# The first unit of a fused attention and expert-mixture kernel: scores copied straight from PSUM, masks on GpSimd, and a new order of the first steps

## The chip, the cores and the metric

The kernel runs on one core of one Trainium2 chip. The metric is the device time of one execution in microseconds (us); three executions give a median of 1105.48 us (1104.85 to 1106.03). All data are fp32.

## The reference

The first block is a recurrent attention. For each of 4 batches and 8 heads a 40 by 40 state is carried over 768 tokens; the second block takes the attention's output, with heads side by side, through four experts and adds them up with weights.

```python
for t in range(S):                                  # S = 768, head_dim = 40
    y[:, :, t] = einsum('bhd,bhde->bhe', r_t, state)
    Sa = einsum('bhde,bhe->bhd', state, a_t)
    state = state * w_t[:, :, None, :] - einsum('bhd,bhe->bhde', Sa, b_t)
    state = state + einsum('bhd,bhe->bhde', v_t, k_t)

x = y as (3072, 320)
p = domain_probs / (domain_probs.sum(-1) + 1e-9)    # 4 experts
for e in range(4):
    out += p[:, e] * (relu(x @ w1[e]) @ w2[e])      # 320 -> 1024 -> 320
```

## The kernel before

**Units.** The tokens are cut into 12 chunks of 64, and the four batches into two pairs. One chunk of one pair is a unit, so there are 24 units, numbered u = 0 to 23; one unit gives 128 rows of x. The recurrence within a chunk is turned into small matrix products and one triangular solve for each head.

**The steps of a unit.** `within(q)` is a generator; each `run(ws[u], 1)` takes it to its next `yield`. It transposes the decays into `G`, scans them, transposes them back by TensorE (`pg`), divides (`gp`, a VectorE reciprocal), scales `n_tok`, `k_tok` and `AT`, transposes the first two by TensorE (`pNT`, `pKT`), and forms the score products `pfe` (for the solve), `pe` (masked into `ET`) and `pc` (masked into `VC`). `pev` multiplies `ET` with the values. `substitute(q, eng)` is the triangular solve: `blocks` gathers the 32 by 32 diagonal blocks of the scores, one VectorE transpose lays them out as `M`, and a loop over 16 pairs of columns fills `Z`. Units 0 and 1 solve on VectorE, later ones on GpSimd. `merge(q)` transposes the result into `Qc` and `QTc`, and joins blocks by the products `pY` and `pQ`. `step(q, xT)` then uses the carried state: products `psat`, `pst`, `pxr`, `pdy`, the output `Y`, the next state, and `pxT`, which places the 40-wide heads into the rows `xT` of x.

**The mixture.** `mixture_of_unit(q)` puts pieces into the list `todo`: `ups(e)` (x times w1 into `ph`, 64 matmuls of 128 columns and four activations to `hs`) and `down(e)` (`po`, 16 matmuls of 320 columns, and one VectorE addition into `osb`). `mix(n)` issues the next n pieces. They are the bulk of TensorE's work, and from the second unit on they fill its waits. Weights come by `load_piece()` (w1, in pieces that alternate over buffers) and `load_w2(e)`.

**What sets the order.** A list scheduler places the instructions of each engine. `tc.keep_in_program_order(ins)` ties an instruction behind the one traced before it on its engine. While `in_order[0]` is set (units 0 to 5), every matmul and transpose is tied, so TensorE runs exactly in the order in which the code calls `run`, `mix` and `keep_warm`. `keep_warm(n)` issues n products of the identity with itself, whose result nobody reads. The order of the first two units is written out by hand at the end of the kernel; SyncE's loads stand there too.

**PSUM.** Tiles by the tag `big` share five banks, those by `mm` three. Before, the target of `keep_warm` is a `big` tile.

The order by hand that the change touches, from the first unit's scores to the second unit's solve, cut to its TensorE and VectorE work, before the change:

```python
run(ws[0], 2); keep_warm(12)                     # scores of unit 0
substitute(units[0], nc.vector, scores_of(0))    # scores_of: masks ET
run(ws[0], 1); m, s = merge(units[0]), begin_step(0)
run(m, 1); run(ws[0]); keep_warm(4); run(norm, 1)
run(ws[1], 1); keep_warm(3); run(ws[1], 1); run(m)
run(ws[1], 1); run(s, 3); run(ws[1], 1); run(s, 1)
run(ws[1], 1); run(s); run(ws[1], 2); mixture_of_unit(units[0])
substitute(units[1], nc.vector, scores_of(1), during_second)
# during_second: mix(1) at j = 0 and 14, the rest of ws[1] at j = 4
```

Of the kernel before, what the change touches and what calls it, by code (L numbers as in the profile page):

```python
# [15 lines left out]
def kernel(  # L16
# [218 lines left out]
    def go(moves, eng=None):  # L235
        for move in moves:
            move(eng or nc.sync)
# [10 lines left out]
    tc.keep_in_program_order(nc.vector.tensor_copy(out=mask_up[:], in_=upf[:]))  # L248
    ins = nc.vector.transpose(out=unit_cols[:], in_=dealt(diagf[:, None, :].to_broadcast([P, H, Q])))
    tc.keep_in_program_order(ins)  # L250
    go(load_raw(units[0], "W"))
    load(units[0], "WBK")
    go(load_raw(units[0], "A"), nc.scalar)
    for x in "VR":
# [82 lines left out]
    def quarter(q):  # L337
        return slice(Q * q, Q * q + Q)
# [63 lines left out]
    def within(q):  # L402
# [3 lines left out]
        def pin(ins, also=False):  # L406
            if q.u <= PADDED or also:
                tc.keep_in_program_order(ins)
# [2 lines left out]
        G = sb.tile([P, 2 * NJ * L + 1], FP32, name="G", tag="G", bufs=3)  # L411
        q.G = Gv = G[:, 0:2 * NJ * L].rearrange("p (c t) -> p c t", t=L)
        ahead = G[:, 1:2 * NJ * L + 1].rearrange("p (j i t) -> p i j t", i=2, t=L)
        for i in range(2):
            pin(turn_raw(ahead[:, i], n["rawW"][:, NJ * i:NJ * i + NJ, :]))
        q.gl = sb.tile([P, 2 * NJ, 1], FP32, name="gl", tag="gl", bufs=4)
        pin(nc.vector.tensor_tensor(out=q.gl[:], in0=G[:, L::L][:, :, None], in1=first[:, :, 0:1], op=ALU.mult))
        pin(nc.vector.memset(Gv[:, :, 0:1], 0.0))
        q.AT = sb.tile([P, 2 * NJ, L], FP32, name="AT", tag="AT", bufs=2)

        def turn_rv():
# [11 lines left out]
            return VT  # L433

        if q.u == 1:
            yield
            VT = turn_rv()
            yield
        pin(nc.vector.tensor_tensor_scan(
            out=G[:, 0:2 * NJ * L], data0=G[:, 0:2 * NJ * L],  # L440
            data1=first[:].rearrange("p c i -> p (c i)"), initial=0.0, op0=ALU.mult, op1=ALU.add,
        ))
        nc.vector.tensor_tensor(out=q.gl[:], in0=q.gl[:], in1=Gv[:, :, L - 1:L], op=ALU.mult)
        if q.u < 2:
            pin(turn_raw(q.AT[:], n["rawA"][:]))
        yield

# [12 lines left out]
        def token_V():  # L460
            return n["paddedV"][:, :, 0:D] if q.u < PADDED else n["V"][:]

        def causal_scores(VT):
            pc = quadrants(banks("pc"), 0, BY_TOKENS, L, lambda j, s, i: (
                d_half(j, s), i, j, of_slots(VT, d_half(j, s), j, i, D), of_slots(q.RT, d_half(j, s), j, i, D),
            ))
            for r in range(2):
                pin(causal(of_d_half(q.VC[:, :, D:D + L], r), pc[r]), q.start)

        q.K, q.N = k_tok(), n_tok()  # L470
        ins = nc.vector.scalar_tensor_tensor(
# [9 lines left out]
        pin(ins)  # L481
        q.VC = VCs()
        if q.u > 0:
            nc.scalar.copy(out=q.VC[:, :, 0:D], in_=token_V())
        if q.u >= PADDED:
            VT = turn_rv()
        yield
# [13 lines left out]
            s, i ^ s, j, of_slots(q.AT, s, j, i), of_pairs(NT, s, j, i),  # L501
        ))
        def copy_F():
            q.F = sb.tile([P, H, L], FP32, name="F", tag="F", bufs=1)
            for s in range(2):
                nc.scalar.copy(out=of_slot(q.F[:], s), in_=pf[s])  # L506
# [13 lines left out]
            yield  # L520

        ET = ETs()
        for s in range(2):
            pin(causal(of_slot(ET[:], s), pe[s]), q.start)
        yield

# [9 lines left out]
        yield  # L536

        if q.u == 0:
            causal_scores(turn_rv())
        yield  # L540

    def substitute(q, eng, between=None, during=None):

        blocks = sb.tile([P, H, Q], FP32, name="blocks")
        for i in range(P // Q):
            move = nc.scalar.copy if i >= 2 else nc.vector.tensor_copy
            tc.keep_in_program_order(move(out=blocks[quarter(i)], in_=q.F[quarter(i), :, quarter(i % 2)]))  # L547
        q.below = belows()
        for i in (1, 3):
            tc.keep_in_program_order(nc.gpsimd.tensor_copy(out=q.below[quarter(i)], in_=q.F[quarter(i), :, 0:Q]))  # L550
        M = sb.tile([P, Q, Q], FP32, name="M")
        cols = blocks[:].rearrange("p h c -> p c h")[:, :, None, :].to_broadcast([P, Q, 4, H])
# [5 lines left out]
        on_diag = M[:].rearrange("p c r -> p (c r)")[:, Q + 1::2 * (Q + 1)]  # L558
        tc.keep_in_program_order(nc.vector.memset(on_diag, 0.0))

        Z = sb.tile([P, 4, Q // 4, Q], FP32, name="Z")
        q.Z = Z[:, 0]
        by_second = Z[:, 1:3].rearrange("p x k r -> p (x k) r")
        below = M[:].rearrange("p c r -> p (c r)")[:, 1::2 * (Q + 1)]
# [4 lines left out]
        ins = nc.vector.tensor_tensor(out=pairs[:, :, 0, :], in0=pairs[:, :, 0, :], in1=by_second, op=ALU.add)  # L569
        tc.keep_in_program_order(ins)  # L570
        run(between)
        at_once = eng is nc.vector
        for x in (0, 3) if at_once else (0,):
            tc.keep_in_program_order(eng.tensor_copy(out=Z[:, x], in_=unit_cols[:]))
        for j in range(0, Q, 2):
            if during:
                during(j)
# [21 lines left out]
    def merge(q):  # L599


        Qc = sb.tile([P, H, Q], FP32, name="Qc", tag="q", bufs=2)
        QTc = sb.tile([P, H, Q], FP32, name="QTc", tag="q", bufs=2)
        tc.keep_in_program_order(nc.vector.transpose(out=dealt(Qc[:]), in_=q.Z))  # L604
        tc.keep_in_program_order(
            nc.vector.transpose(  # L606
                out=QTc[:].rearrange("p h r -> p (h r)"), in_=Qc[:].rearrange("p h c -> p (h c)"),
            )
        )
        q.QT = QTs()  # L610
        for i in range(P // Q):
            ins = nc.gpsimd.tensor_copy(out=q.QT[quarter(i), :, quarter(i % 2)], in_=QTc[quarter(i)])  # L612
            tc.keep_in_program_order(ins)
        yield

        def two_heads(name, lhsT, rhs, to):
            p = big(name)
            for n in range(NJ):
                for r in range(2):
                    matmul(  # L620
                        out=p[half(r), n * 2 * Q:(n + 1) * 2 * Q], lhsT=lhsT[half(r), 2 * n:2 * n + 2, :],
                        rhs=rhs[half(r), 2 * n:2 * n + 2, :], start=True, stop=True,
                    )
            for r in range(2):
                for y in range(2):
                    src = p[quarter(2 * r + y), 0:H * Q].rearrange("p (n two t) -> p n two t", two=2, t=Q)[:, :, y, :]
                    nc.scalar.copy(out=of_slot(to[quarter(2 * r)], y), in_=src)  # L627

        Y = Ys()
        two_heads("pY", q.below, QTc, Y)  # L630
        yield

        two_heads("pQ", Qc, Y, q.QT[:, :, quarter(1)])
        yield

    def step(q, xT):
# [31 lines left out]
        if not q.end:  # L668
# [2 lines left out]
                i ^ s, i, j, q.QT[half(i ^ s), head(j, s), :], RH[half(i ^ s), head(j, s), 0:D],  # L671
            ))
        SaT = sb.tile([P, NJ, 2, L], FP32, name="SaT", tag="step", bufs=3)
        for x in range(2):
            nc.scalar.copy(out=SaT[:, :, x, :], in_=psa[x])
        if not q.end:
            for x in range(2):
                for i in range(2):
                    s = i ^ x
                    nc.scalar.copy(out=of_slot(SX[half(i)], s)[:, :, 0:D], in_=pst[x][half(i)])  # L680
        yield

        p = banks("pxr")
# [34 lines left out]
            )  # L718
        if not q.start:
            nc.vector.tensor_tensor(out=Y[:], in0=Y[:], in1=Gv, op=ALU.mult)  # L720
        if not q.end:
            gl = q.gl[:].rearrange("p (j i) o -> p j i o", i=2)
            for i in range(2):
                x = st[i][:, :, 0:D]
                nc.vector.tensor_tensor(out=x, in0=pdy[i][:, :, 0:D], in1=x, op=ALU.add)
                nc.vector.tensor_tensor(out=x, in0=x, in1=gl[:, :, i, :].to_broadcast([P, NJ, D]), op=ALU.mult)
        yield

        if placed:
# [7 lines left out]
        for h in range(0 if placed else H):  # L737
            lo = h * D
            while lo < (h + 1) * D:
# [7 lines left out]
                    )  # L747
                lo = hi
        yield

    def up_last(k, xT, n):

# [48 lines left out]
    def mixture_of_unit(q):  # L801
# [3 lines left out]
        def ups(e):  # L805
            ph = []

            def lead():
                if not ph:
                    ph.append(up_last(at + 2 * e, q.xT, P))  # L810

            def piece():
                lead()
                hs[e] = [up_main(at + 2 * e, q.xT, P, ph[0])]
                hs[e].append(up_main(at + 2 * e + 1, q.xT, P, up_last(at + 2 * e + 1, q.xT, P)))
                used(at + 2 * e + 2)
                if q.u == 0 and e + 2 < E:
                    load_w2(e + 2)

            piece.lead = lead  # L820
            return piece
# [176 lines left out]
        q.xT = chunks_x[q.c][:, :, q.bp * P:(q.bp + 1) * P]  # L998
        return step(q, q.xT)

    warm = big("warm")

    def keep_warm(n):

        for _ in range(n):
            ins = matmul(out=warm[:, 0:P], lhsT=ident[:], rhs=ident[:], start=True, stop=True)
            tc.keep_in_program_order(ins)

    in_order[0] = True
# [5 lines left out]
    run(ws[0], 1)  # L1015
    keep_warm(10)
    run(ws[0], 1)
    run(ws[1], 1)
    for x in "VR":
        load_padded(units[1], x)  # L1020
    load(units[1], "WBK")
    go(load_raw(units[1], "A"))
    go(load_raw(units[2], "W"))
    load_probs()
    run(ws[0], 2)
    keep_warm(12)

    def scores_of(u):
        run(ws[u], 1)
        yield  # L1030

    substitute(units[0], nc.vector, scores_of(0))
    run(ws[0], 1)
    set_pick()
    m, s = merge(units[0]), begin_step(0)
    run(m, 1)
    run(ws[0])
    keep_warm(4)
    run(norm, 1)
    run(ws[1], 1)  # L1040
    keep_warm(3)
    load(units[2], "W")
    for x in "VR":
        load_padded(units[2], x)
    load_piece()
    load_piece()
    run(ws[1], 1)
    go(load_raw(units[2], "A"))
    load_w2(0)
    load_piece()  # L1050
    load_piece()
    run(m)
    run(ws[1], 1)
    run(s, 3)
    run(ws[1], 1)
    run(s, 1)
    run(ws[1], 1)
    run(s)
    load(units[2], "BK")
    load_w2(1)  # L1060
    load_piece()
    run(ws[1], 2)
    mixture_of_unit(units[0])

    def during_second(j):
        if j in (0, 14):
            mix(1)
        if j == 4:
            run(ws[1])
        if j == 12:  # L1070
            run(norm)

    substitute(units[1], nc.vector, scores_of(1), during_second)
    m, s = merge(units[1]), begin_step(1)
    run(m, 1)
    run(ws[2], 1)
# [144 lines left out]
```

## Time and profile before

| what | value |
|---|---|
| median of three executions | 1105.48 us (1104.85 to 1106.03) |
| the profiled execution, its own time | 1102.3 us |
| its span, first to last instruction | 1100.6 us |
| mean granted TensorE clock | 0.991 |
| TensorE matmuls busy | 1070.0 us (97%) |
| VectorE busy | 756.6 us (69%) |
| ScalarE busy | 353.0 us (32%) |
| GpSimd busy | 502.9 us (46%) |
| stage 0 to 20 us: matmuls busy, clock | 13.59 us, 1.00 |
| stage 20 to 40 us | 13.11 us, 0.65 |
| stage 40 to 60 us | 18.94 us, 0.93 |
| stage 60 to 80 us | 19.13 us, 1.00 |

Times in this text that name a moment are us from the span's start. In lists of instructions the columns are start, length, engine, line and operation, what is written from what, the number of instructions, and in brackets the idle time before the first of them with what ended it. Lines of a table by stage give the stretch, its length, and for each engine the busy time with the number of instructions, then the granted clock, the mean share of the DMA engines and GB/s. The profiled execution lies 3.2 us below the median of the others.

### The profile page before, as it was taken

How to read it: one execution, taken by the hardware profiler on the slowest of the kernel's cores; microseconds unless marked ns; L12 is line 12 of the kernel's file. 1: busy time of each engine (PE TensorE's matmuls, PEld its weight loads, DVE VectorE, ACT ScalarE, POOL GpSimd, SP SyncE). 2: the span in 40 equal slices, each digit the busy share in tenths (PEclk: the TensorE clock that was granted, in tenths of full speed). 3: DMA queues.
4: the chain of work that ended last, by engine and by line, in shares of the span. 5: the costliest groups of instructions: out<-in, count | busy, mean ns of one | idle time of the engine just before them, and what ended most of it. 6: DMA issues, size and time to landing. Idle time of an engine off the chain costs nothing.

```text
span 1100.6 us, 38528 instructions
## 1 busy us (share of the span) xinstructions
PE 1070.0 (97%) x16102; PEld 955.8 (87%) x16102; DVE 756.6 (69%) x1551; ACT 353.0 (32%) x956; POOL 502.9 (46%) x1274
## 2 busy tenths in 40 slices
PE   6799899999999999999999999999999999999998
PEld 6677788789998999898999989989998989988887
DVE  7766668887777776767767768767767677543343
ACT  2432444223233233243233242332332432321110
POOL 5106677753463653743734635636537437430000
PEclk9799999999999999999999999999999999999999
DMA  7776545425345363354353444443552532222320
GB/s 117 226 247 138 136 103 117 119 55 136 98 111 127 98 140 97 94 146 103 93 144 94 102 121 104 116 120 84 127 123 65 147 85 67 98 69 82 104 76 13
DMA packets 268868, 122.18 MB, mean 111 GB/s; under 512 B 213736, under 2 KB 242072, under 8 KB 268696
## 3 DMA queue, kind: packets, MB, share of 16 engines
q1 hardware_dynamic: 265416, 119.12, 43.0%
q8 instruction: 127, 2.08, 0.8%
q10 hardware_dynamic: 3280, 0.61, 0.3%
q14 instruction: 45, 0.37, 0.1%
HBM read 111.79 MB, written 3.93 MB: 105 GB/s over the span
## 4 chain that ended last, share of the span: by engine, by line
PE 81%; DVE 7%; POOL 5%; ACT 3%; issue 2%; DMA 1%; SPq 0%; ACTq 0%; DVEq 0%; POOLq 0%
PE ph L76 35%; PE p L76 28%; POOL Z L593 3%; PE pdy L76 3%; PE psat L76 2%; PE pxr L76 2%; POOL Z L580 2%; PE prn L76 1%; PE pfe L76 1%; PE pQ L76 1%; PE po L76 1%; PE pc L76 1%; DVE Z L590 1%; PE pY L76 1%; DVE M L553 1%
## 5 line engine op out<-in xcount | busy, mean ns | idle before, releaser
L76 PE MATMUL ph<-xT,w1p 128*128 128x256 f32 (+3 forms) x3040 | 446.3, 377 | 4.0 <-issue 3.9
L76 PEld LDWEIGHTS ph<-xT,w1p 64*64 64x64 f32 (+1 forms) x3040 | 338.5, 162 | 72.7 <-issue 29.0
L593 POOL TENSOR_TENSOR Z<-Z 128x31 f32<-128x31 f32 (+7 forms) x704 | 260.0, 369 | 55.2
L897 DVE TENSOR_TENSOR a<-hs 128x512 f32<-128x512 f32 x220 | 151.8, 707 | 104.7 <-ACT hs L778 104.7
L580 POOL TENSOR_TENSOR Z<-M,Z 128x62 f32<-128x62 f32 (+7 forms) x352 | 144.1, 409 | 132.3 <-DVE M L569 106.4
L778 ACT ACTIVATE hs<-ph 128x512 f32<-128x512 f32 (+1 forms) x208 | 115.3, 564 | 226.5 <-PE ph L76 225.4
L76 PE MATMUL p<-sums,a 128*128 128x160 f32 x1056 | 164.9, 299 | 0.0
L76 PEld LDWEIGHTS p<-sums,a 128*128 128x128 f32 x1056 | 152.8, 190 | 2.2
L791 DVE SCALAR_TENSOR_TENSOR osb<-p,gate,osb 128x320 f32<-128x320 f32 (+1 forms) x243 | 108.1, 481 | 57.8 <-PE p L76 53.6
L550 POOL COPY below<-F 32x256 f32<-32x256 f32 x48 | 22.8, 475 | 198.7 <-ACT F L506 197.0
L76 PE MATMUL p<-w,a 128*128 128x160 f32 x704 | 105.9, 301 | 0.2 <-ACT hs L778 0.2
L76 PE MATMUL p<-w,hs 128*128 128x160 f32 x704 | 102.9, 299 | 0.0
L76 PEld LDWEIGHTS p<-w,hs 128*128 128x128 f32 x704 | 100.2, 190 | 2.2
L76 PEld LDWEIGHTS p<-w,a 128*128 128x128 f32 x704 | 98.3, 190 | 3.0 <-ACT hs L778 3.0
L612 POOL COPY QT<-QTc 32x256 f32<-32x256 f32 x96 | 51.7, 539 | 76.9 <-DVE QTc L606 67.7
L553 DVE STREAM_TRANSPOSE M<-blocks 128x1024 f32<-128x1024 f32 x24 | 47.4, 1977 | 38.1 <-ACT blocks L547 37.9
L700 ACT COPY RS<-pxr 64x256 f32<-64x256 f32 x88 | 32.2, 366 | 105.2 <-DVE SX L400 43.1
L451 DVE RECIPROCAL gp<-gp 128x320 f32<-128x320 f32 x24 | 51.6, 2151 | 0.7
L535 ACT COPY EV<-pev 64x160 f32<-64x160 f32 x96 | 23.1, 286 | 89.7 <-PE pev L76 89.3
L604 DVE STREAM_TRANSPOSE Qc<-Z 128x256 f32<-128x256 f32 x24 | 15.0, 627 | 46.2 <-POOL Z L593 46.1
L627 ACT COPY QT<-pQ 32x128 f32<-32x128 f32 x96 | 24.6, 256 | 59.9 <-PE pQ L76 58.2
L659 ACT COPY SN<-prn 128x256 f32<-128x256 f32 x44 | 14.9, 372 | 78.6 <-DVE RH L654 78.6
(149 smaller groups left out, 1357.5 us busy)
## 6 DMA issues: line engine op xcount, KB each, us to landing
w1p<-in_moe_w_dram SPq DMA_DIRECT2D x95, 512.0 KB
w1p<-in_moe_w_dram SPq DMA_DIRECT2D x190, 64.0 KB
w<-in_moe_w_dram SPq DMA_DIRECT2D x4, 1280.0 KB
sums<-in_moe_w_dram SPq DMA_DIRECT2D x9, 512.0 KB
natW<-in_w_dram SPq DMA_DIRECT2D x48, 80.0 KB
natB<-in_b_dram SPq DMA_DIRECT2D x48, 80.0 KB
natK<-in_k_dram SPq DMA_DIRECT2D x48, 80.0 KB
out_dram<-osb SPq DMA_DIRECT2D x46, 80.0 KB
```

What stands on the lines that cost most here:

```text
L76: return stated(nc.tensor.matmul(**k))
L451: pin(nc.vector.reciprocal(out=gp[:], in_=gp[:]))
L535: nc.scalar.copy(out=of_slot(q.EV[half(p)], i ^ p)[:, :, 0:D], in_=pev[i][half(p)])
L553: ins = nc.vector.transpose(out=M[:], in_=cols)
L580: ins = eng.tensor_tensor(out=Z[:, 1:3, 0:n, j + 1:Q], in0=M[:, j:j + 2, None, j + 1:Q].to_broadcast([P, 2, n, m]), in1=Z[:, here, 0:n, j: ...
L593: eng.tensor_tensor(out=z[:, 0], in0=z[:, 0], in1=z[:, x], op=ALU.add)
L612: ins = nc.gpsimd.tensor_copy(out=q.QT[quarter(i), :, quarter(i % 2)], in_=QTc[quarter(i)])
L627: nc.scalar.copy(out=of_slot(to[quarter(2 * r)], y), in_=src)
L700: nc.scalar.copy(out=RS[half(s), x ^ s::2], in_=prs[x][half(s)].rearrange("p (j i) t -> p j i t", i=2),)
L778: nc.scalar.activation(out=h[:, i * HF // 2:(i + 1) * HF // 2, 0:n], in_=ph[i][:], func=ACTF.Relu,)
L791: nc.vector.scalar_tensor_tensor(out=to, in0=p, scalar=sc, in1=to, op0=ALU.mult, op1=ALU.add)
L897: nc.vector.tensor_tensor(out=t[:], in0=x, in1=y, op=op)
```

## The change

1. The four loads of the first unit's decays alternate between SyncE's queue and ScalarE's queue, ahead of the other loads there.
2. `within` turns the second unit's `V` and `R` first, its decays in the next step and `AT` in a third, before the scan, and has one more `yield`.
3. Units 0 and 1 have no SBUF copy `F` of their scores. `blocks` is copied from the PSUM banks `pf` in eight parts (five by VectorE, three by ScalarE), and `below` by four ScalarE copies in place of two GpSimd copies from `F`.
4. In unit 0 the two masks (`ET` and the right half of `VC`) are no longer predicated VectorE copies. ScalarE copies the scores to SBUF, and GpSimd's `affine_select` writes them masked (`selected`).
5. In unit 0 the two copies of the unit columns into `Z` stand ahead of the gathering of `blocks` instead of after the masks.
6. In unit 0 half of the copies out of `pY`, `pQ`, `psat` and `pst` go to VectorE.
7. The next state of unit 0 is computed in a step of its own, later.
8. The spare products write a tile of the tag `mm`, and there are 16, 10, 19, 5, 8 and 6 of them where there were 16, 10, 12, 4 and 3.
9. The order by hand changes. The first unit's masks, its `V` and `R`, the gate's transposes and the second unit's `V` and `R` are all called ahead of the first `merge`. The second unit's scan stands behind the whole first step; the first piece of the mixture, `ups(0)`, stands ahead of the second unit's `n_tok`, and no longer inside its solve. Loads move with it: the third unit's decays go behind two weight pieces.

```diff
-    go(load_raw(units[0], "W"))
+    for n, move in enumerate(load_raw(units[0], "W")):
+        tc.keep_in_program_order(move(nc.scalar if n % 2 else nc.sync))
...
         if q.u == 1:
+            VT = turn_rv()
             yield
-            VT = turn_rv()
+        for i in range(2):
+            pin(turn_raw(ahead[:, i], n["rawW"][:, NJ * i:NJ * i + NJ, :]))
+        if q.u == 1:
+            yield
+            pin(turn_raw(q.AT[:], n["rawA"][:]))
...
+        def selected(to, spread, data):
...
+            for s in range(2):
+                tc.keep_in_program_order(nc.scalar.copy(out=spread(copied, s), in_=data[s]))
+            for i in range(2):
+                nc.gpsimd.affine_select(
+                    out=to[part(i)], in_=copied[part(i)], pattern=[[0, H], [1, L]], compare_op=ALU.is_gt, fill=0.0,
+                    base=0, channel_multiplier=-1,
+                )
...
+        if q.u == 0:
+            unit_columns()
+        if q.pf:
+            for n, (i, s) in enumerate((i, s) for i in range(P // Q) for s in range(2)):
+                move = nc.scalar.copy if n >= 5 else nc.vector.tensor_copy
+                to, src = of_slot(blocks[quarter(i)], s), q.pf[s][quarter(i), :, quarter(i % 2)]
+                tc.keep_in_program_order(move(out=to, in_=src))
+            if q.u > 0:
+                copy_below(q)
...
-    warm = big("warm")
+    warm = ps.tile([P, P], FP32, name="warm", tag="mm", bufs=3)
...
     run(ws[0], 2)
-    keep_warm(12)
-
-    def scores_of(u):
-        run(ws[u], 1)
-        yield
-
-    substitute(units[0], nc.vector, scores_of(0))
-    run(ws[0], 1)
     set_pick()
+    keep_warm(19)
+    substitute(units[0], nc.vector)
+    run(ws[0], 3)
+    keep_warm(5)
+    run(ws[0])
+    run(norm, 1)
+    keep_warm(8)
+    run(ws[1], 1)
+    keep_warm(6)
     m, s = merge(units[0]), begin_step(0)
     run(m, 1)
-    run(ws[0])
-    keep_warm(4)
-    run(norm, 1)
-    run(ws[1], 1)
-    keep_warm(3)
...
     run(ws[1], 1)
+    go(load_raw(units[2], "W"))
+    run(m, 1)
+    run(ws[1], 1)
...
     run(m)
-    run(ws[1], 1)
-    run(s, 3)
+    run(s, 4)
     run(ws[1], 1)
     run(s, 1)
     run(ws[1], 1)
+    mixture_of_unit(units[0])
+    mix(1)
+    run(ws[1], 1)
     run(s)
+    run(ws[1], 1)
...
     run(ws[1], 2)
-    mixture_of_unit(units[0])
...
     def during_second(j):
-        if j in (0, 14):
-            mix(1)
         if j == 4:
             run(ws[1])
         if j == 12:
             run(norm)
+        if j == 14:
+            mix(1)
```

## The prediction

> **What bounds the kernel now.** I read the page first, then the table by stage, then the instructions of each engine over the first 75 us.
>
> ```profile
> PE 1070.0 (97%) x16102; PEld 955.8 (87%) x16102; DVE 756.6 (69%) x1551; ACT 353.0 (32%) x956; POOL 502.9 (46%) x1274
> ...
> PEclk9799999999999999999999999999999999999999
> ```
>
> TensorE is 97% busy and its clock is low in one slice, the second (27.5 to 55 us). From about 75 us the order of the work is unchanged, so the change is worth what it moves the moment at which unit 2's first product, `pg`, can start behind the same pieces of the mixture. Now that is 69.75. The table by stage (stretch, length, busy and count of PE, PEld, DVE, ACT, POOL, clock, DMA share, GB/s):
>
> ```profile
> 18.00:20.30 2.30, 0.00 (x1) 0.03 (x1) 2.15 (x6) 0.00 (x0) 0.00 (x0) 1.00 0.71 129
> 22.50:36.10 13.60, 8.19 (x72) 6.98 (x74) 12.03 (x35) 4.38 (x13) 2.40 (x4) 0.50 0.60 145
> 36.10:39.50 3.40, 2.49 (x36) 1.80 (x35) 0.58 (x2) 2.05 (x8) 0.00 (x0) 0.99 0.63 112
> 39.50:43.00 3.50, 3.05 (x95) 2.76 (x96) 2.81 (x4) 1.79 (x6) 1.30 (x2) 0.51 1.00 355
> 48.50:54.30 5.80, 5.23 (x81) 4.58 (x72) 4.64 (x9) 2.98 (x8) 0.84 (x2) 1.00 0.84 231
> 54.30:69.75 15.45, 14.95 (x128) 11.15 (x128) 14.28 (x50) 2.49 (x8) 2.26 (x4) 1.00 0.74 232
> ```
>
> Up to 48.5 TensorE waits for VectorE's chain, with a halved clock for 17 us; after it TensorE has 0.6 + 0.5 us idle up to 69.75. VectorE's list gives the first solve:
>
> ```profile
> 13.61 0.92 DVE L241 STREAM_TRANSPOSE G<-rawW 128x256 f32<-128x256 f32 x2
> ...
> 16.21 1.99 DVE L553 STREAM_TRANSPOSE M<-blocks 128x1024 f32<-128x1024 f32 x1 [0.16 <-ACT blocks L547]
> ...
> 19.73 0.76 DVE L400 COPY_PREDICATED ET<-mask_up,pe 128x256 f32<-128x256 int32 x2
> 20.39 0.49 DVE L574 COPY Z<-unit_cols 128x256 f32<-128x256 f32 x2
> 20.80 0.22 DVE L580 TENSOR_TENSOR Z<-M,Z 128x62 f32<-128x62 f32 x1
> ```
>
> and TensorE's list the waits behind it:
>
> ```profile
> 32.98 1.11 PE L79 MATMUL pRT<-ident,padded 128*128 128x128 f32 x4 [3.83 <-DVE VC L400]
> 33.88 1.49 PE L76 MATMUL warm<-ident 128*128 128x128 f32 x6
> ...
> 48.55 2.60 PE L76 MATMUL ph<-xT,w1p 64*64 64x128 f32 x32
> ...
> 54.32 1.00 PE L76 MATMUL pev<-VC,ET 64*64 64x40 f32 x32 [0.58 <-DVE ET L400]
> ...
> 69.75 0.66 PE L79 MATMUL pg<-ident,G 128*128 128x128 f32 x4 [0.47 <-DVE G L439]
> ```
>
> `QTc` is done at 32.60, yet `pY`, which needs it, starts at 35.30: `pRT` waits for a bank that the mask `VC` frees, and three spare products follow.
>
> **Part by part, to the first piece of the mixture.** (1) Loads: SyncE's four issues now end at 2.79 and `G` starts 5.76. Two on SyncE, the first held to 1.45 by the memset of `rawW`, end at 1.45 + 2 x 0.45 = 2.35. From the end of issue to landing the chain shows 2.33 us (`rawW` of unit 1) and 3.08 (`rawA`): start at 4.7 to 5.4. I take 4.7, the row of the same tensor: -1.05. `rawA` moves 0.9 us back on ScalarE's queue, to about 6.2, needed at 7.5: hidden. (2) `blocks`: from the end of `pfe` (14.63) to `M` is 1.58 us now. After: five VectorE copies of 32x128 from PSUM, each between 0.17 (a 128x8 operation) and 0.34 (32x256 from SBUF); nearest is 0.31 for 128x160 from PSUM, overlapping to one per 0.25, so 1.3 us; three on ScalarE at 0.26 end sooner. -0.3 (0 to -0.6). (3) The mask and the unit columns between `M` and the loop go: 20.80 - 19.73 = -1.07. The columns (0.49) are covered by the gap at 13.6 that unit 1's two `G` transposes leave; without it they cost 0.49. (4) Four GpSimd selects of 64x512: between 0.29 (a 128x128 select) and 1.27 (a two-input 128x512 operation); I take 0.7. Two of them fall in the loop. Beside set-up selects VectorE's `AT` multiplication took 0.77 instead of 0.69; beside GpSimd's own multiplication at 42.5 its `n_tok` took 1.22 instead of 0.49. I take the first, the row of a select: some 0.2 us over the loop (0 to 1.4).
>
> The Trainium skill, "SBUF — State Buffer", section "Terms", has GpSimd and VectorE lock a shared port pair for a whole instruction, the loser fully blocked. By that rule both selects would stop the loop, 1.4 us and not 0.2; the row of 0.77 against 0.69 speaks for less.
>
> So `QTc` ends at 32.60 - 1.05 - 0.3 - 1.07 + 0.2 = 30.4. (5) TensorE before it, from the end of `pe` (14.1): 38 spare products at 2.94/12 = 0.245 us, 9.3; `pev` 0.9, `pc` 1.0, five transposes 3.2: 14.4, done by 28.5, so `pY` starts at 30.5. Nothing queued behind these waits is late: ScalarE's copies out free the banks, `below`'s four (1.05 us) lie under `M`, and `set_pick` on GpSimd ends at 15.1 as before. On SyncE's queue the loads of unit 2's decays (2.27 us of issue, at 19.87 now) go behind the first two weight pieces, which are issued from 28.5 now and from about 25 then, needed at 40; behind the decays, held until `G` of unit 1 is read at 31.4, w2 of the first expert comes at about 35.7 (now 37.4), needed only at 54: hidden.
>
> (6) The step, at full clock, by rows of this or a later unit: `pY` 0.6, `Yq` on two engines 0.55, `pQ` 0.7, `QT` 0.6 (GpSimd's four `QT` copies, 2.54 us from 30.4, end together with it), `psat` 0.75, `SaT` 0.4, `pxr` 0.7, half of the `SX` mask 0.45, `pdy` 1.75, `Y` 0.8, `pxT` 1.5, copy `xT` 0.55: 9.35 with hand-overs up to 9.6. `ph` starts at 40.1, against 48.55. That is a lead of 8.45 us. The next state, moved out, is about 1.1 us of VectorE work in a later wait.
>
> **What is given back.** (7) `ups(0)` (5.19 us) now stands ahead of `pNT`, `pKT` (1.1) and `pc`, `pfe`, `pe` (1.63) of unit 1. VectorE's scan, `gp`, reciprocal and `n_tok` (1.3 + 0.5 + 2.15 + 0.5 after `Y`) and GpSimd's `k_tok`, `AT` (0.86 + 1.27) end at 45.4, just when `ups(0)` does; covered. `pe` of unit 1 ends at 40.1 + 5.2 + 2.7 = 48.0, against 48.74. (8) What is late next: `pev` needs `ET`, which stands behind `blocks` and `M`. `pe` to `M` is 1.61 us now, 1.35 after; `M` to `pev` 3.97. So `pev` starts at 53.3, and TensorE has nothing queued for 5.3 us, where `ups(0)` stood before. (9) From `pev` to the end of `down(1)` takes 15.0 us (54.32 to 69.29): 68.3. (10) VectorE's side: `pe` to scan of unit 2 is 20.96 us now, 20.7 after: 68.7. (11) The clock: at 207.47 TensorE idled 2.09 us and then ran at half speed from 210.2 to 213.6, losing 1.7 us:
>
> ```profile
> 209.56 6.38 PE L76 MATMUL ph<-xT,w1p 64*64 64x256 f32 x30 [2.09 <-issue]
> ...
> 210.00:213.75 3.75, 3.75 (x19) 2.52 (x11) 3.72 (x9) 0.00 (x0) 3.23 (x5) 0.54 0.70 119
> ```
>
> An idle time of 5.3 us will do the same: one window of 3.4 us at half speed, 1.7 us, at most 2.7 (1.6 windows), at least 0.75. So `pg` of unit 2 starts at 68.3 + 1.7 = 70.0, against 69.75: +0.25. The lead of 8.45 us is spent on 2.7 of unit 1's products, 5.3 of idle, 1.7 of clock, less the 1.1 idle of before. The profiled execution would take 1102.3 + 0.25; it lies 3.2 below the median, so the median goes from 1105.48 to 1105.7.
>
> The Trainium skill, "TensorE: Matmul & The Clock Gate", section "HAM oscillation — how this bites in real kernels", asks only for no idle gaps over about 3.4 us. By it the gaps of 0.5 to 0.8 us in the new step would be harmless. The rows say otherwise: 36.1 to 39.5 has 0.9 us idle in pieces, and the next 3.5 us ran at 0.51.
>
> **The rivals.** (B) Faster by over 0.2% (2.2 us; 0.2% is about what a measurement of this kernel can tell from no change). The idle time costs no clock, VectorE's 68.7 decides (-1.05), and the stalls of the old stream that nothing explains, 1.32 us at 124.30 and 2.09 at 207.47 with 1.7 of clock, move with the 19 more spare products; losing the larger gives -1.05 - 3.8 = -4.8, half of it -3.0, near 1102.5. For it: both stand in `ph`, after dense small products. Against: the new dense stretch at 33 to 37 can stall likewise. (C) Slower: the halved clock also meets the step. Its products on the path are some 6 us at full clock, two thirds of the time, so each window of 3.4 us at half speed there costs about 1.0; two of them, and a second one after the idle time, give 0.25 + 2.0 + 1.7 = +3.95, near 1109.4. It decides from the second extra window. For it: the same step runs at 0.51 now. Against: 38 spare products keep TensorE busy up to 28.5. (D) The select path does not take the masks off the path: if selects stop the loop in full and `QTc` comes 2.8 us later (four of 0.7), everything follows: +3.0, near 1108.5.
>
> **How the numbers follow.** The forecast, no difference: 0.37; its own range, from the clock's bounds and +-1.2 for steps 1 to 6, is 1103.3 to 1107.7. B 0.32, C 0.27, D 0.04. The range reaches to B's -4.2 and C's +4.3: 1101.3 to 1109.8. Faster 0.32, same 0.37, slower 0.31.
>
> **What would show it.** Right: `G` at 4.7, first loop at 18.4, `pY` near 30.5, `ph` near 40, an idle TensorE of about 5 us before unit 1's `pev` with 0.5 in the clock after it, `pg` of unit 2 near 70. Wrong: `ph` before 38 or after 42; a full clock through `down(0)`; `pg` before 67.5 or after 72.

## The result and the profile after

The changed kernel takes 1110.02 us (median of seven executions, 1108.17 to 1113.64), the kernel before 1103.86 (1103.05 to 1106.03, seven executions beside it): a ratio of 1.0056, 95% interval 1.0038 to 1.0074. It is slower by 6.2 us; the forecast was no difference. The profiled execution took 1113.64 us, the slowest of the seven, with a span of 1111.6; so its loss of clock is larger than usual, and sizes read from it are compared below with other runs.

The page of after, the lines of TensorE and of its clock:

```profile
PE 1079.4 (97%) x16140; PEld 965.4 (87%) x16140; DVE 757.3 (68%) x1560; ACT 352.2 (32%) x959; POOL 503.4 (45%) x1274
...
PEclk9789999999999999999999999999999999999999
```

The work is the same but for the spare products; the low clock is still there. The first solve in VectorE's list of after:

```profile
5.28 0.93 DVE L241 STREAM_TRANSPOSE G<-rawW 128x256 f32<-128x256 f32 x2 [1.53 <-DMA rawA<-in_a_dram]
...
13.01 0.71 DVE L587 COPY Z<-unit_cols 128x256 f32<-128x256 f32 x2
14.09 1.29 DVE L596 COPY blocks<-pfe 32x128 f32<-32x128 f32 x5 [0.37 <-PE pfe L76]
15.88 2.00 DVE L608 STREAM_TRANSPOSE M<-blocks 128x1024 f32<-128x1024 f32 x1 [0.49 <-ACT blocks L596]
...
19.52 0.22 DVE L633 TENSOR_TENSOR Z<-M,Z 128x62 f32<-128x62 f32 x1
```

The mask and the unit columns are gone from between `M` and the loop, and the loop starts at 19.52 instead of 20.80. `M` waits for ScalarE: its three copies of `blocks` came after VectorE's five, not beside them. TensorE's list of after:

```profile
31.47 0.68 PE L76 MATMUL pY<-QTc,below 64*64 64x64 f32 x16 [3.17 <-DVE QTc L659]
...
47.18 2.65 PE L76 MATMUL ph<-xT,w1p 64*64 64x128 f32 x32
...
54.44 0.68 PE L76 MATMUL pfe<-AT,KT 64*64 64x64 f32 x32
61.07 1.42 PE L76 MATMUL pev<-VC,ET 64*64 64x40 f32 x32 [5.96 <-DVE ET L401]
62.42 7.15 PE L76 MATMUL po<-w,hs 128*128 128x320 f32 x16
...
78.88 0.60 PE L79 MATMUL pg<-ident,G 128*128 128x128 f32 x4
```

`pY` starts 3.8 us sooner than before (35.30), `ph` only 1.4 sooner (48.55), and unit 2's `pg` 9.1 later (69.75). The row `pfe<-AT,KT` is unit 1's last score product, which the prediction calls `pe`; it ends at 55.12, against 48.74 before:

```profile
48.09 0.65 PE L76 MATMUL pfe<-AT,KT 64*64 64x64 f32 x32
```

The table by stage of after (columns as before):

```profile
28.35:31.47 3.12, 0.00 (x1) 0.03 (x1) 2.88 (x11) 0.47 (x2) 0.08 (x1) 1.00 0.91 287
31.47:47.18 15.71, 13.02 (x208) 11.59 (x208) 7.33 (x22) 2.90 (x9) 1.49 (x4) 0.57 0.79 226
47.18:55.10 7.92, 7.88 (x169) 7.01 (x168) 3.92 (x5) 2.96 (x7) 2.33 (x2) 1.00 0.30 46
55.10:61.07 5.97, 0.01 (x2) 0.03 (x1) 5.19 (x11) 1.51 (x7) 0.00 (x0) 0.69 1.00 327
61.07:69.50 8.43, 8.43 (x48) 5.71 (x48) 7.11 (x28) 0.95 (x4) 0.00 (x0) 0.61 1.03 309
```

An idle TensorE (0.00 and 0.01 us busy) in the first and the fourth row, a low clock (0.57 and 0.61) in the row behind each. The stall at 207 of before is still there, 10 us later:

```profile
219.85 6.42 PE L76 MATMUL ph<-xT,w1p 64*64 64x256 f32 x30 [2.10 <-issue]
```

### The profile page after: what moved, and what is told of

It is laid out like the page before. It is cut to its first block, busy times and chain, and to the rows that moved or that the text cites. A ratio compares the mean times of both kernels' runs of the same rounds, so it can differ in the third digit from the quotient of the medians.

```text
span 1111.6 us, 38612 instructions
## 1 busy us (share of the span) xinstructions
PE 1079.4 (97%) x16140; PEld 965.4 (87%) x16140; DVE 757.3 (68%) x1560; ACT 352.2 (32%) x959; POOL 503.4 (45%) x1274
## 4 chain that ended last, share of the span: by engine, by line
PE 76%; DVE 6%; POOL 5%; SPq 4%; ACT 3%; DMA 3%; issue 2%; ACTq 0%; DVEq 0%; POOLq 0%
PE ph L76 33%; PE p L76 26%; POOL Z L646 3%; SPq L223 3%; PE pdy L76 3%; PE psat L76 2%; PE po L76 2%; POOL Z L633 2%; PE pxr L76 2%; PE prn L76 1%; PE pQ L76 1%; PE pfe L76 1%; PE pc L76 1%; PE pev L76 1%; DVE M L608 1%
## 5 line engine op out<-in xcount | busy, mean ns | idle before, releaser
L646 POOL TENSOR_TENSOR Z<-Z 128x31 f32<-128x31 f32 (+7 forms) x704 | 255.4, 363 | 55.2
L633 POOL TENSOR_TENSOR Z<-M,Z 128x62 f32<-128x62 f32 (+7 forms) x352 | 148.9, 423 | 132.9 <-DVE M L623 107.0
```

Source lines behind the costliest of these rows:

```text
L633: ins = eng.tensor_tensor(out=Z[:, 1:3, 0:n, j + 1:Q], in0=M[:, j:j + 2, None, j + 1:Q].to_broadcast([P, 2, n, m]), in1=Z[:, here, 0:n, j: ...
L646: eng.tensor_tensor(out=z[:, 0], in0=z[:, 0], in1=z[:, x], op=ALU.add)
```

## The experiments

The theories. **1, the clock:** the halved clock in the step and in `down(0)` is the loss. **2, idle time:** the wait before `pev` is the loss, because `ups(0)` no longer fills it. **3, shared copies:** copies that two engines share take turns and lengthen the chain. **4, unit 1's order:** its scan and scores come too late; what counts is when its last score product ends, since VectorE's chain of some 21 us from there sets unit 2's `pg`.

**More spare products.** Three kernels: 18 instead of 6 ahead of the first merge; 24 ahead of unit 1's `pev`; both.

```diff
-    keep_warm(6)
+    keep_warm(18)
     m, s = merge(units[0]), begin_step(0)
...
     run(ws[1], 2)
+    keep_warm(24)
```

> The changed kernel with 18 instead of 6 spare products ahead of the first merge, so that TensorE is busy from 28.3 to 31.3, where it idled 3.2 us. Theory 1 (the clock): the step after it ran at 0.50 of the clock from 33.8 to 47.1 because of that idle time; with it filled the step runs at full clock, the first piece of the mixture starts at 42 to 43 instead of 47.2, and the median falls by 3 to 5 us, to 1105 to 1107. Theory 2 (only the order of the pieces and the idle time before the second unit's pev cost): no difference, 1109 to 1111. Theory 3 (the copies shared with VectorE cost the time, by waiting in turn): no difference either.

> The changed kernel with 24 spare products between the second unit's pe and pev, where TensorE idled 6.0 us (55.1 to 61.1). Nothing useful is moved. Theory 1 (the clock): po after it took 7.1 us at a halved clock and takes 4.5 us now; VectorE's chain then decides, near 76.5 for unit 2's pg against 78.9, so 2 to 3 us faster, 1107 to 1108. Theory 2 (the idle time itself, the work missing there): no difference, since the spare products do no work.

> Both fillings of spare products in one kernel (18 ahead of the first merge, 24 between the second unit's pe and pev), so that TensorE has no long idle time up to unit 2's pg. Theory 1 (the clock is the whole loss): the clock stays up, and the median falls to that of before, 1103 to 1105. Theory 4, formed after the first runs (the second unit's scores come late, and VectorE's chain of 21.5 us from them to unit 2's pg decides): the spread of the runs shrinks to some 2 us, since the clock is out of it, but 4 to 5 us over before stay: 1107 to 1109.

The first: 1112.81 us, ratio 1.0077 (1.0059 to 1.0095), no gain where theory 1 had 1105 to 1107. In its profiled execution (1108.44 us, the fastest of six, mean clock 0.994) the step ran at full clock, and the idle time before `pev` still halved it for `po` (5.86 us); the other five show a mean clock of 0.988, and no profile tells where they lost it. The second: 1110.13, 1.0064 (1.0041 to 1.0087), no gain either. Both together: 1107.12, 1.0030 (1.0018 to 1.0042), 2.9 us under the changed kernel, and still 3.2 over before, as theory 4 had it (1107 to 1109); all eleven executions have a mean clock of 0.995 or more. In that last kernel the clock is whole in the step, in the former idle time and in `po`:

```profile
31.40:44.20 12.80, 9.79 (x220) 8.32 (x219) 7.54 (x23) 2.90 (x9) 1.57 (x4) 1.00 0.80 220
52.70:58.70 6.00, 5.52 (x49) 5.36 (x49) 5.27 (x11) 1.51 (x7) 0.00 (x0) 1.00 1.02 336
58.70:64.00 5.30, 5.25 (x48) 3.69 (x48) 4.92 (x20) 0.95 (x4) 0.00 (x0) 1.00 1.05 298
```

and its TensorE list shows what is left:

```profile
44.20 2.65 PE L76 MATMUL ph<-xT,w1p 64*64 64x128 f32 x32
...
51.98 0.68 PE L76 MATMUL pfe<-AT,KT 64*64 64x64 f32 x32
...
74.15 0.66 PE L79 MATMUL pg<-ident,G 128*128 128x128 f32 x4 [0.49 <-DVE G L444]
```

Here `pg` waits for VectorE's scan `G`, not for the mixture: 21.5 us after the last score product (52.65). So theory 1 holds for about half of the loss, if both gaps are closed. The spare products themselves ran past the end of the wait, so that `pY` starts at 32.57 and not 31.47; about 1 us of what is left may be theirs.

**Filling the wait before `pev`.** `ups(0)` back into unit 1's solve; the same with the weight loads moved along; and `norm` with `down(0)` at the loop's start instead.

```diff
-    mixture_of_unit(units[0])
-    mix(1)
...
-    used(2)
-    load_w2(2)
+    load_piece()
...
+    mixture_of_unit(units[0])
...
+        if j == 0:
+            mix(1)
+            used(2)
+            load_w2(2)
```

> The changed kernel with one part undone: the first piece of the mixture is called inside the second unit's solve again, at j = 0, and not ahead of n_tok. Theory 2 (the order): the idle time before pev is filled by 5.2 us of work, TensorE waits some 3 us for n_tok instead, unit 2's pg starts 4 us earlier, 1105 to 1107. Theory 1 (the clock, in the first step): the step at half speed stays, since the idle time at 28.3 does; of the loss some 3 us remain, so not below 1105.

> The changed kernel with the first piece of the mixture called inside the second unit's solve again, with the weight loads that follow it moved along, so that its weights stand. Theory 4: pe of the second unit is no longer behind 5.2 us of ph, but it still waits for n_tok behind the whole first step; pe ends some 2 to 3 us earlier and unit 2's pg with it: 1106 to 1108. Theory 1: the idle time moves from ahead of pev to ahead of pNT (3.3 us) and costs clock as before: no gain, 1109 to 1111.

> The changed kernel with the second piece, down(0), called at j = 0 of the second unit's solve, ahead of pev, and the gate's normalisation ahead of it, so that the idle 6.0 us hold 4.5 us of work. Theory 2 (work missing there): TensorE gains 4.5 us and 2.6 of clock, but VectorE's chain from pe to the scan of unit 2, 21.3 us, allows only 2.4: 1107 to 1108. Theory 1 says the same from the clock alone, so this run against the one with spare products tells whether work or VectorE's chain decides: equal times mean VectorE.

The first left the loads where they were, so `ups(0)` read pieces that held other weights, and TensorE waited 9.71 us for a transfer: 1116.9 us, 1.0118 (1.0103 to 1.0132), which says nothing on theory 2. The second: 1110.34, 1.0062 (1.0042 to 1.0081), no better than the changed kernel, as theory 1 had expected; theory 4's 1106 to 1108 missed. The wait was filled, but a new one came ahead of unit 1's scores, and again VectorE's scan was last:

```profile
49.17 0.66 PE L79 MATMUL pNT<-ident,n_tok 128*128 128x128 f32 x4 [3.30 <-DVE n_tok L492]
...
74.66 0.66 PE L79 MATMUL pg<-ident,G 128*128 128x128 f32 x4 [0.47 <-DVE G L444]
```

The third: 1113.04, 1.0075 (1.0059 to 1.0091), where both theories had 1107 to 1108; `pg` at 78.55 after 6.29 us of waiting for VectorE. Theory 2 falls: with the wait filled by work, VectorE still sets the end.

**The banks.** A kernel, run once, in which `blocks` is split by PSUM bank (s = 0 VectorE, s = 1 ScalarE), and the copies of `Yq` and `QT` by partitions of one bank.

```diff
-                move = nc.scalar.copy if n >= 5 else nc.vector.tensor_copy
+                move = nc.scalar.copy if s else nc.vector.tensor_copy
...
-                    if q.u == 0 and y:
+                    if q.u == 0 and r:
```

> One look at what makes two engines take turns. The copies out of pY and pQ are shared by halves of the partitions (one bank, separate parts of the output), those of blocks by bank (two banks, interleaved outputs). If the order comes from the PSUM bank, the copies out of pY still go in turn, about 1.26 us from first to last, and those of blocks run side by side, some 1.1 us instead of 1.8. If it comes from the output, it is the other way round: 0.6 us for pY and 1.8 for blocks.

It took 1110.11 us. VectorE's list and then ScalarE's:

```profile
14.40 1.19 DVE L596 COPY blocks<-pfe 32x128 f32<-32x128 f32 x4 [0.36 <-PE pfe L76]
...
32.98 0.60 DVE L682 COPY Yq<-pY 32x128 f32<-32x128 f32 x2 [0.67 <-ACT Yq L684]
```

```profile
14.44 1.06 ACT L596 COPY blocks<-pfe 32x128 f32<-32x128 f32 x4 [0.35 <-PE pfe L76]
...
32.37 0.52 ACT L684 COPY Yq<-pY 32x128 f32<-32x128 f32 x2 [1.65 <-PE pY L76]
```

From two banks they start together; from one bank VectorE waits until ScalarE is through, also where their partitions differ. In this program, two engines do not read one bank side by side. The Trainium skill, "PSUM — Partial Sum Buffer", section "Terms", calls two engines at once on the same bank and the same quadrant of 32 partitions an error; the rows show this program keeping them apart between quadrants of one bank as well.

**Unit 1's old order.** The changed kernel with unit 1's calls in the order of before (scan ahead of the step's products, `n_tok` ahead of `pxT`, `ups(0)` in the solve) and the first unit's copies by ScalarE alone; then the same with `osb`'s first addition tied to the solve's eighth pair.

```diff
     load_piece()
-    run(ws[1], 1)
+    run(ws[1], 2)
...
     run(m)
-    run(s, 4)
     run(ws[1], 1)
-    run(s, 1)
+    run(s, 3)
     run(ws[1], 1)
-    mixture_of_unit(units[0])
-    mix(1)
+    run(s, 1)
```

```diff
-            if j == 0:
+            if j == 0 or (q.u == 1 and j == 14):
                 tc.keep_in_program_order(ins)
...
-            add(q.osb[:], po[:], scale(q, e), e == 0)
+            ins = add(q.osb[:], po[:], scale(q, e), e == 0)
+            if q.u == 0 and e == 0:
+                tc.keep_in_program_order(ins)
```

> The changed kernel with the second unit's order of before (scan ahead of the first step, its pg after pQ, n_tok ahead of pdy, ups(0) in the solve) and with all copies out of pY, pQ, psat and pst on ScalarE; what stays is the first unit's shorter chain. Theory 4: pY starts at 31.5 against 35.3 of before, the second unit's pe ends at 46 to 47 against 48.7, and unit 2's pg comes 2 us earlier than before: 1102 to 1103, faster than before by 0.1 to 0.2%. Theory 1: the idle time at 28.3 still halves the clock in the step, so 1105 to 1107. Theory 3 (the shared copies cost most): the same gain as theory 4 predicts, so the trace has to tell: the copies out of pY and pQ took 1.26 us each and take 1.07 us here, which is 0.4 us of it.

> The first unit's shorter chain with unit 1's old order (its scan before the first step, its n_tok before the products into pdy, the first ups beside unit 1's solve, the first unit's copies all by ScalarE), as in the run before, but with VectorE's first addition into osb held at the eighth pair of the solve's loop, so that the mm bank of down(0) comes free there. If the lead of some 4 us is lost because unit 1's scores are moved behind the whole step (theory 4): pe(1) ends at 44.6 to 46.5, VectorE's chain of 21 us from there ends at 66 to 67.5, and pg(2) starts at 67 to 68.5 (69.75 before); 1101.5 to 1103.5 us, faster than before by 0.5 to 2.5. If the halved clock in the step alone is what costs (theory 1): the spare products before pY are the same, so the step lies at half clock in some executions, and the time is 1105 to 1108. If the shared copies were the loss (theory 3): they are gone here too, so this run does not tell 3 from 4.

The first missed what every theory had for it: 1110.6 us, 1.0061 (1.0046 to 1.0077). The scheduler had put the addition behind the whole loop (it starts at 67.30), so that the `mm` bank of `down(0)` stayed occupied:

```profile
57.78 2.65 PE L76 MATMUL ph<-xT,sums 64*64 64x128 f32 x32
67.88 1.23 PE L76 MATMUL ph<-xT,sums 64*64 64x128 f32 x16 [7.45 <-DVE osb L858]
```

With that one instruction tied: 1102.4 us, 0.9986 (0.9975 to 0.9998), 7.6 under the changed kernel, and a little under before, though by less than the 0.2% that a measurement tells apart. Its TensorE list:

```profile
46.70 0.35 PE L76 MATMUL pfe<-AT,KT 64*64 64x64 f32 x3 [2.11 <-issue]
46.83 4.24 PE L76 MATMUL ph<-xT,w1p 64*64 64x128 f32 x32
...
68.98 0.66 PE L79 MATMUL pg<-ident,G 128*128 128x128 f32 x4 [0.76 <-DVE G L444]
```

The last score product ends at 47.05, and `pg` follows 21.9 us later. It would have ended some 2 us sooner without a stall for which the profile shows no releaser. TensorE idles 3.19 us ahead of `pY` here as in after, but the half clock behind it lasts 3.4 us and not 13.7, and the executions have a mean clock of 0.992 to 0.995 (after: 0.986 to 0.992): so a part of what the old order gains is clock, and theories 1 and 4 do not add up as separate shares.

**Two by two: order and copies.** The changed kernel with the old order and the tied addition, but its shared copies; and with its own order, but ScalarE's copies.

```diff
-                    if q.u == 0 and y:
+                    if False:
...
-            if q.u == 0 and x:
+            if False:
```

> The changed kernel with nothing undone but the order of unit 1 (its scan and gp before the first step's products, its n_tok before pxT, the first ups beside its solve, VectorE's first addition into osb held at the eighth pair of the loop). Against the kernel of three runs before that had this order (1102.4) it has the shared copies back: two of Yq, two of QT, one of SaT and two of SX by VectorE. If the order carries the whole loss (theory 4): 1102 to 1103.5, within 1 us of that kernel, some 7 us under the changed kernel; pY's first copies to psat take 0.2 to 0.6 us longer, and unit 1's scan stands behind the copies of Yq. If the shared copies carry part of it (theory 3): 1103.5 to 1105, 1 to 2.5 us over that kernel, ph 1 to 2 us later than its 46.83.

> The changed kernel with its own order of unit 1 and only the shared copies undone: Yq, QT, SaT and SX of the first unit all by ScalarE. So far: changed order and shared copies 1110.0, old order and shared copies 1105.65, old order and ScalarE's copies 1102.4. If the shared copies cost by themselves (theory 3): 1106.5 to 1108, about 3 us under the changed kernel, as with the old order. If they cost only where unit 1's scan and reciprocal stand in front of them on VectorE, that is, if the change moved the scan to make room for them (theory 4 with this as its reason): within 1 us of the changed kernel, 1109 to 1111, or up to 2 us over it, as ScalarE's eight more copies stand in a row between pst and pxr.

| | copies shared | copies by ScalarE |
|---|---|---|
| changed order | 1110.02 us, 1.0056 (1.0038 to 1.0074) | 1109.26, 1.0048 (1.0029 to 1.0067) |
| old order | 1105.65, 1.0021 (1.0010 to 1.0031) | 1102.4, 0.9986 (0.9975 to 0.9998) |

The diff leads from the left column to the right one; each ratio is against runs of before on the same chip. The cell of the old order with shared copies lies over what either theory had (1102 to 1105); that of the changed order with ScalarE's copies came as theory 4 had it (1109 to 1111), and not as theory 3 (1106.5 to 1108). Taking the shared copies away gains less than 1 us in the changed order and 3.2 us in the old one. A reason is in VectorE's list of the lower left cell, with ScalarE's copy of the other half of `SaT` below it:

```profile
34.81 1.22 DVE L444 TENSOR_TENSOR_SCAN G<-G,first 128x512 f32<-128x512 f32 x1
...
36.28 0.28 DVE L682 COPY QT<-pQ 32x128 f32<-32x128 f32 x1
...
37.83 2.15 DVE L456 RECIPROCAL gp<-gp 128x320 f32<-128x320 f32 x1
39.90 0.36 DVE L733 COPY SaT<-psat 128x256 f32<-128x256 f32 x1
```

```profile
38.37 0.37 ACT L735 COPY SaT<-psat 128x256 f32<-128x256 f32 x1 [1.53 <-PE psat L76]
```

The copies that the first unit's chain needs stand behind unit 1's scan and reciprocal. Its step also ran at half clock for 13.7 us (32.9 to 46.6), and how the 3.2 us divide between the two is not shown. So the shared copies go better with that scan moved away, and moving it away is what costs.

One length runs through the profiles. From the end of unit 1's last score product to unit 2's `pg` it is 21.0 us before, and 21.4 to 23.8 in every kernel but the two in which TensorE waited 7.45 and 9.71 us in between. That product ends at 48.74 before, at 51.7 to 55.9 in the eight kernels with the scan behind the step, also with a whole clock (52.65), and at 45.7 to 50.0 in the four with the old order and the tied addition. This is what theory 4 says.

**A better version.** The old order with ScalarE's copies and 18 spare products, and this with `blocks` split by bank.

> The same with 18 instead of 6 spare products ahead of pY, so that TensorE is not idle for 3 us there. Theory 1 (clock): 1 to 3 us less than the kernel of the run above and a smaller spread. Theory 4 (unit 1's order): the same as the run above to within 1 us, pg(2) at 67 to 68.5. If both hold: pg(2) at 67 to 68.5 in every execution, 1100.5 to 1103 us.

> The same as the run above, and the eight blocks split by PSUM bank (s=0 by VectorE, s=1 by ScalarE) in place of five and three: M is written some 0.2 to 0.5 us sooner, so pY and all behind it up to pe(1) lie 0.2 to 0.5 us sooner and the time is 0.2 to 0.5 us less, which is near what can be told; if the banks do not matter, no difference.

1103.82 us, 0.9998 (0.9986 to 1.0011), and 1103.0, 0.9995 (0.9979 to 1.0012, single executions from 1097.8 to 1107.47): no gain over the kernel with 6 spare products there, and no difference between the two that the intervals tell. In their profiled executions `pg` starts at 68.40 and 67.20, as early as in no other kernel, and this does not reach the end. In all three of these kernels 70 to 120 us has a clock of 0.97, where before has 1.00: one stretch of 3.4 us at half clock (105.0 to 108.4 with 6 spare products), behind a wait of 1.78 us for VectorE that ends at 104.23. Before has the same wait, up to 104.97, and keeps its clock, so what decides was not isolated.

## Why the prediction was wrong

The step that failed is step 6, the first unit's step from `pY` to `ph`: 9.6 us in the sum, 11.6 us measured at a whole clock, and 12.3 to 16.2 in kernels of this order and these copies without more spare products ahead of it. With it unit 1's scores, called behind the step, come too late, and step 10 was too short to show what that costs.

That times follow unit 2's `pg` held roughly. Own time less start of `pg` is 1032.6 for the profiled execution of before, 1034.8 for after, and 1031 to 1036 for the other kernels. The clock in the 100 us behind `pg` goes with it: in before and the other kernels where it is whole there, the difference is 1031.1 to 1032.6, in the others, at 0.96 to 0.98, 1032.9 to 1035.8. So most of the error is in the 70.0 against 78.88, step by step:

- **Steps 1 to 5: 1.0 us late** (`QTc` at 31.33 for 30.4). `G` gained 0.48, not 1.05: SyncE's queue issued `natW` (0.80) ahead of its two `rawW` (1.62 to 2.71). `blocks` lost 0.3 instead of gaining it: from `pfe` to `M` 1.84 us, for 1.58 before and 1.3 in the sum, as the copies took turns. The mask and the columns gained 0.95 for 1.07 (`M` to the loop 3.64 us, 4.59 before). The fill of TensorE (28.3 for 28.5) was right, and so were the selects, 0.69 to 0.74 us each; the loop took 11.81 us (19.52 to 31.33) against 11.80 before, with two selects in it (24.38 to 25.85). The rule of "SBUF — State Buffer" in the Trainium skill, section "Terms", weighed there at 1.4 us, does not show in the length of the loop.
- **Step 6, the one that failed: 15.7 us from `pY` to `ph`, not 9.6.** At full clock it takes 11.6 (the kernel with both sets of spare products, 32.57 to 44.20), so 2.0 us were mis-sized and 4.1 are clock. Of the 2.0, `pY` to `psat` has 0.7 (3.15 us for 2.45): `Yq` took 1.26 us by turns, more than ScalarE's 1.07 alone. `psat` to `pxr` has 0.75 (1.90 us for 1.15): `QT`, by turns, is complete only 0.8 us behind `psat`'s start. The sum took a whole clock for the step, though its plan has TensorE idle ahead of `pY` (28.5 to 30.5; 3.17 us measured); only rival C prices that.
- **Step 7** was right in length: `ph` to the end of `pe` 7.94 us for 7.9. **Step 8:** 5.95 us for 5.3, mostly the turns again (`pe` to `M` 1.83 for 1.35).
- **Steps 9 and 11:** `pev` to `pg` took 17.8 us, for 15.0 and 1.7 of clock. The clock cost about 2.8 (`po` 7.15 for 4.57), the upper end given (2.7).
- **Step 10** was too short: with VectorE setting the end, 21.4 us or more from unit 1's last score to `pg`, for 20.7 to the scan. With the scores as late as step 6 makes them, this puts `pg` at 74.15 even with a whole clock. The comparison never made was with the old order on the shorter chain, where `pe` ends before `ups(0)` begins.
- **Rival C** had the mechanism for the clock, but only about half of the loss is its. That its 1109.4 is near is in part luck: it adds 3.95 to a median of 1105.48 from three executions, and against the 1103.86 of seven the loss is 6.2. The order was in no rival.

The 4.1 us of clock belong to the slowest execution. The kernel with split banks, 1110.11 us, has the order and the shared copies of after and no more spare products: its step takes 12.3 us (31.65 to 43.95), and `pg` starts at 74.35. Of these 4.35 us over 70.0, step 6 has 2.7 and steps 1 to 5 have 1.15. So step 6 leads in both, and in an execution near the median its size at a whole clock weighs more than the clock.

The rule of "TensorE: Matmul & The Clock Gate" ("HAM oscillation — how this bites in real kernels"), no gaps over some 3.4 us, would have passed the 3.17 us ahead of `pY`. The rows of after show a clock of 0.57 behind it: the gap was enough, as in the six other kernels with the same gap (last section).

## What to carry to other kernels

A lead on one engine's chain is worth only what the next chain can start on. Before a unit's work is moved behind another's to free an engine, follow the chain that the moved work feeds: here, at a whole clock, `ph` came 4.4 us sooner (44.20 for 48.55) and the second unit's last score product 3.9 us later (52.65 for 48.74). In these runs, copies shared by two engines ran side by side only from different PSUM banks, and those that stood behind long work on one engine came late. An idle time that the plan itself shows wants a price: here 3.2 us ahead of the step cost it 3.4 to 17 us at half clock. When an order is undone, look where the scheduler then puts each untied instruction; one addition was worth 8 us here.

## What the runs showed of the hardware

The wait ahead of `pY` decides whether the step loses its clock. Seven profiled executions idle 3.17 to 3.21 us there, and all seven fall to half clock at 30.7 to 33.5. Three idle 1.40 to 1.53 us, and fall to it later, at 35.2 to 35.6. Four idle 0.48 us or less, and keep the whole clock through the step; one of them at 76% busy (9.79 of 12.80 us, above).

The half clock lasts 3.4 us or a multiple of it, here once to five times. In after it lasted four times, with TensorE 77% to 100% busy:

```profile
33.50:36.90 3.40, 2.97 (x59) 2.76 (x60) 1.38 (x5) 0.56 (x3) 0.00 (x0) 0.50 0.69 125
36.90:40.30 3.40, 2.95 (x84) 2.66 (x81) 1.84 (x5) 0.90 (x3) 0.00 (x0) 0.50 0.92 255
40.30:43.70 3.40, 2.61 (x52) 2.29 (x45) 1.04 (x3) 0.46 (x1) 0.00 (x0) 0.50 1.05 360
43.70:47.10 3.40, 3.40 (x16) 3.15 (x16) 1.84 (x6) 0.48 (x1) 0.00 (x0) 0.50 0.59 178
```

The same step won its clock back after one such stretch in the kernel with split banks, and with the old order in the one at 1102.4 us:

```profile
35.25:38.65 3.40, 3.25 (x95) 2.95 (x94) 1.54 (x5) 0.95 (x3) 0.00 (x0) 0.50 0.69 131
```

```profile
33.20:36.60 3.40, 3.29 (x61) 2.84 (x64) 2.24 (x4) 1.11 (x6) 0.00 (x0) 0.50 0.69 121
```

So the same step can hold a whole clock at a busy share (76%) at which it stayed at half clock in after (77%, 87%). But the share alone does not settle it: every stretch at half clock that was 95% busy or more was the last of its row in these profiles, while among those at 77% to 94% both occur (before won its clock back at 87%, 39.6 to 43.0).
